# One multiplication of the score preparation on GpSimd, the state's decay behind two copies, and two buffers in place of three for a chunk's closing outputs

## The chip, the cores and the metric

The kernel runs on one core of a Trainium2 chip. The time is the device time of one execution in microseconds (us); the figure that counts is the median of several executions. Engines are called as the profile calls them: PE is the matrix engine, DVE the vector engine, ACT the scalar engine, POOL is GpSimd, SP the engine whose queue issues nearly all DMA transfers.

## The reference

Three stages follow each other: a recurrent attention with a decaying state, and two gated networks without a nonlinearity.

```python
# r, k, v: 4 x 8 x 768 x 48 (batch, head, time, dim);  w, u: 8 x 48
for t in range(S):
    cur = einsum('bhd,bhe->bhde', u[None] * kt, vt)
    y[:, :, t] = einsum('bhd,bhde->bhe', rt, state + cur)
    state = w[None, :, :, None] * state + einsum('bhd,bhe->bhde', kt, vt)
x = y as 3072 rows of 384
x = (x @ w_a * (x @ w_b)) @ w_out          # block 1: 384 -> 1536 -> 384
x = ((x @ w1 * (x @ w2)) @ w3) @ w_out2    # block 2: 384 -> 1024 -> 1024 -> 384
```

## The kernel before, in words

**Stages.** Time is cut into 6 chunks of 128 steps; a chunk of one batch row is a unit, so there are 24 units, unit u being row `u % 4` of chunk `u // 4`. A unit's attention is done in chunk form: r times powers of w (table `tr`) and k times inverse powers (`tk`) give scores by matmul; scores are masked, the diagonal gets the term with u, and the masked scores (`a_sc`) times v, plus r times the state, give y. Chunk 0 (units 0 to 3) has no state to add. For chunks 0 and 1 the preparation is `prep_0` with three multiplications of 112x512 each: part 0 is k times the table (L599), part 1 is r times the table (L602), part 2 is e = r times k (L604). They read the loaded tile `rk` and write the unit's tile `alt`. A part-1 result is wanted by the score matmuls (`scores_h`, L365 and L369), a part-2 result by the diagonal's matmuls (`scores_d`, L377, with a filler matmul L286 behind them). From chunk 2 on, L333 and L338 multiply `rk` in place on POOL.

**A unit's tail.** DVE masks the scores (L389 in chunks 0 and 1, `a_mask` later), ACT copies the part below without a mask (`h_off`, L397; from chunk 2 on `a_off`, L440, twice in a unit). Then y (L479 and L484, later `y_split`, L456), the state's sum over the chunk (L569), the state's decay by w to the 128th on ACT (`s_decay`, L576, four instructions) and the state's update on DVE (L589).

**Block 1.** A finished chunk of y (`xt`) goes through block 1 in 12 column blocks f: nine matmuls L641 for a and nine for b into PSUM banks `ab0` to `ab2`; ACT copies a into an SBUF buffer `g0`, `g1` or `g2` (L745); DVE multiplies (L746); ACT and DVE split the product in a high and a low part (L748, L751); 27 matmuls (L658 to L660) add it to the banks `m0` to `m2`. After the last f `m_close` empties the three m banks into three buffers of the same `g0` to `g2` (L720 on ACT; for chunk 0, which is done in two parts around chunk 1, L718 on DVE adds the kept part), and SP sends each to DRAM (`m_d`, L723). The weights arrive as 64-bit floats and are converted on DVE and ACT (L976, L980, L984, L989, L992, from tile `raw` to `wab`, `wo`).

**Block 2** runs after chunk 5, in another part of the program (L1202 to L1400), and the change does not touch it.

**What sets the order.** Nothing is ordered by hand: each step is a task with an engine, an assumed duration, dependences, buffers and a priority, and `plan` lays the tasks out by list scheduling on assumed times; each engine's instructions then stand in the program in that order. A DVE task marked `sbuf=True` is assumed longer while POOL is busy. A changed dependence or duration therefore also reorders work that it does not name.

```python
        if t.sbuf:
            t.dur += max(0.0, min(free.get("POOL", 0.0) - at, 2 * t.dur)) / 2
```

Of the kernel before, what the change touches and what calls it, by code (L numbers as in the profile page):

```python
# [13 lines left out]
ALU = mybir.AluOpType  # L14
# [4 lines left out]
B, H, S, D = 4, 8, 768, 48  # L19
# [149 lines left out]
def rwkv_moe_kernel(ctx, tc, rkT, nat, wu, wab, wout, w12, w3T, wo2, r_in, k_in, v_in, w_in, u_in, out):  # L169
# [10 lines left out]
    def flat(ap):  # L180
        return ap.rearrange("p a b -> p (a b)")

    with tc.manual_schedule():
# [411 lines left out]
        def prep_0(u, part):  # L595
            rk, t = rk_t[u], alt[u % B]
            rf_t[u] = t[0:112, 0].rearrange("p (n c) -> p n c", n=NP)
            if part == 0:
                nc.vector.tensor_tensor(out=t[0:112, 1].rearrange("p (n c) -> p n c", n=NP),  # L599
                                        in0=rk[:, 1, :].rearrange("p (n c) -> p n c", n=NP), in1=tk, op=ALU.mult)  # L600
            elif part == 1:
                nc.vector.tensor_tensor(out=t[0:112, 0], in0=rk[:, 0, :], in1=flat(tr), op=ALU.mult)  # L602
            elif part == 2:
                nc.gpsimd.tensor_tensor(out=t[0:112, 2], in0=rk[:, 0, :], in1=rk[:, 1, :], op=ALU.mult)  # L604
            else:
                nc.scalar.copy(out=vz_t[u % 2][:, :, :, D:],
                               in_=v_0[:, u, 6 * D:].rearrange("p (x k i) -> p k x i", x=2, k=KD))
# [64 lines left out]
        def task(*a, **k):  # L672
            t = Task(*a, **k)
            for b in t.bufs:
                b.users.append(t)
            tasks.append(t)
            return t

        def use(t, *bufs):
            for b in bufs:  # L680
                b.users.append(t)
            return t
# [172 lines left out]
        for u in range(B, NU):  # L855
            c, b = divmod(u, B)
            pu = due(28 + 8 * (u - B)) if c == 1 else due(125 + 20 * (u - 2 * B)) if c == 2 else -1000.0 + 10 * u
            rk_b[u], nat_b[u] = Buf(rk_s, none), Buf(nat_s, none)
            lr = task("SP", 0.4, lambda u=u: load_rk(u), [], pu - 100, [rk_b[u]], size=0.45)
            ln = task("SP", 0.4, lambda u=u: load_nat(u), [], pu - 100, [nat_b[u]], size=0.39 if c == 1 else 0.58)  # L860
            at_c = at_s + banks
            ba = Buf(a_s, none)
            kn = []
            if u == 2 * B:
                bt = Buf(at_c, none)
                tn = use(task("PE", 0.9, lambda bt=bt: picked([bt], tables_s), s_kn, due(82), [bt]), tmp_b)
                tn = use(task("ACT", 0.6, tables_n, [tn], due(82)), bt)
            if c < NC - 1:
                bk = Buf(kn_s, none)
                eng, d = ("DVE", 0.55) if c == 1 else ("POOL", 1.15)  # L870
                kn = s_kn = [use(task(eng, d, lambda u=u: k_nat(u), [ln, tn] + s_kn, pu, [bk]), nat_b[u])]
            if c == 1:
                bt, bd = [Buf(at_c, none) for _ in range(2)], Buf(at_c, none)
                al = alt_b[b]
                pu_ = use(task("POOL", 1.3, lambda u=u: prep_0(u, 2), [lr], pu - 9), rk_b[u], al)
                pk = use(task("DVE", 0.7, lambda u=u: prep_0(u, 0), [lr], pu - 9, sbuf=True), rk_b[u], al)
                pr = use(task("DVE", 0.7, lambda u=u: prep_0(u, 1), [lr, pk], pu - 9, sbuf=True), rk_b[u], al)
                sc = use(task("PE", 1.2, lambda u=u, bt=bt: picked(bt, lambda: scores_h(u)), [pk, pr] + after, pu, bt), al)
                sd = use(task("PE", 0.85, lambda u=u, bd=bd: picked([bd], lambda: scores_d(u)), [sc, pu_], pu, [bd]), al)
                ev = halves(u, pu - 60, sc, sd, bt, bd, ba)  # L880
                by = [Buf(at_c, none)]
                y = use(task("PE", 2.3, lambda u=u, by=by: picked(by, lambda: y_mm(u)), ev + s_up.get(u - B, []), pu + 1, by),
                        al, nat_b[u], ba)
                bs = [Buf(at_c, none)]
                sm = use(task("PE", 0.6, lambda u=u, bs=bs: picked(bs, lambda: s_mm(u)), kn + [y], pu + 2, bs), bk, nat_b[u])
                after = [y, sm]
                s_old, s_new = y, sm
            else:
                al = rk_b[u]
                t = use(task("POOL", 1.32, lambda u=u: prep_r(u, nc.gpsimd), [lr], pu - 9), rk_b[u])  # L890
                t = use(task("POOL", 1.32, lambda u=u: prep_k(u, nc.gpsimd), [t], pu - 9), rk_b[u])
                bp = Buf(pr_s, none)
                dg_b[u] = Buf(dg_s, none)
                d = use(task("POOL", 1.15, lambda u=u: prep_d(u, 0), [ln, load_u], pu - 8, [bp]), nat_b[u])
                d = use(task("POOL", 1.15, lambda u=u: prep_d(u, 1), [d], pu - 8), nat_b[u], bp)
                dg = use(task("DVE", 0.56, lambda u=u: prep_d(u, 2), [d], pu - 8, [dg_b[u]]), bp)
                by, bt = [Buf(at_s, none) for _ in range(2)], [Buf(banks, none) for _ in range(2)]
                sc = use(task("PE", 1.5, lambda u=u, bs=by + bt: picked(bs, lambda: state_scores(u)),
                              [t] + after + s_up.get(u - B, []), pu, by + bt), rk_b[u])
                of, ev = [], []  # L900
                for x in range(2):
                    ev = [use(task("DVE", 0.42, lambda u=u, x=x: a_mask(u, x), [sc] + ev, pu - 300, [] if x else [ba]), bt[x], ba)]
                    of.append(use(task("ACT", 0.28, lambda u=u, x=x: a_off(u, x), ev, pu - 300), bt[x], ba))
                ev = use(task("DVE", 0.77, lambda u=u: a_diag(u), ev + [dg], pu, sbuf=True), ba, dg_b[u])
                y = use(task("PE", 1.4 if kn else 1.1, lambda u=u: y_split(u), [ev] + of + kn, pu + 1), al, nat_b[u], ba, *by)
                if kn:
                    use(y, bk)
                after, bs = [y], by
                s_old, s_new = sc, y
            if b == 0:  # L910
                x_b[c] = Buf([x_s[X_TAG[c]]], none)
                y3_b[c] = Buf(y3_s, none)
                x_in[c] = []
            ev_y = []
            for g, d in ((None, 0.9),) if c == 1 else ((1, 0.52), (0, 0.4)):
                take = [x_b[c], y3_b[c]] if b == 0 and not ev_y else []
                yh = use(task("ACT", d, lambda u=u, g=g: y_evac_h(u, g), [y] + ev_y, pu + 2, take), by[g or 0], x_b[c], y3_b[c])
                yr = [yh]
                if c == 1:
                    yr = [use(task("PE", 0.3, lambda u=u: y_rest(u), [yh], pu + 2), by[0], x_b[c], y3_b[c])]  # L920
                yl = use(task("DVE" if c > 1 else "ACT", d, lambda u=u, g=g: y_evac_l(u, g), yr + ev_y[1:], pu + 2), by[g or 0], x_b[c], y3_b[c])
                ev_y = [yh, yl]
                x_in[c].append(yl)
            if c < NC - 1:
                sd = task("ACT", 1.56, lambda u=u: s_decay(u), [s_old], pu + 3)
                s_up[u] = [use(task("DVE", 0.85, lambda u=u: s_upd(u), [s_new, sd] + ([] if c == 1 else ev_y), pu + 3), *bs)]
            if b == B - 1:
                x_in[c].append(use(task("SP", 0.4, lambda c=c: y_shuffle(c), list(x_in[c]), pu + 3, size=0.13),
                                   x_b[c], y3_b[c]))
# [96 lines left out]
        for n, (q, fs) in enumerate([(0, range(SPLIT)), (1, range(NF1)), (0, range(SPLIT, NF1))]  # L1026
                                    + [(q, range(NF1)) for q in range(2, NB)]):
            mb = Buf(m_s, none)
            base, step = ((due(30), 80.0), (due(75), 66.0), (0.0, 10.0))[min(n, 2)]
            base += 200.0 * max(0, n - 2)  # L1030
            t_ab, t_m = block1(q, fs, base, step, x_b[q], x_in[q], mb, [m_last] if n else [])
            m_last = t_m[fs[-1]]
            if n:
                d = m_close(q, m_last, mb, base + 15 * step, g_s, g_get)
            else:
                d = [use(task("ACT", D_A, lambda k=k: m_keep(0, k), [m_last], base + 5 * step), mb) for k in range(KD)]
            if n == 2:
                mp.users = d
# [666 lines left out]
```

## Time and the profile before

| what | value |
| --- | --- |
| runs | 859.61, 860.3, 862.42 us; median 860.3 us |
| profiled execution | 860.08 us, of which the span from the first to the last instruction is 858.4 us |
| PE busy | 845.4 us of the span |
| DVE, ACT, POOL busy | 573.3, 401.2, 199.1 us |
| mean granted clock of PE | 0.998 |

The span leaves PE 13.0 us without a matmul. The 1.7 us between the span and the run's time lie outside the instructions. "Granted clock" is the share of PE's full speed that the chip granted.

### The profile page before, as it was taken

The numbers are of one execution on the slowest core, as the hardware profiler recorded it, in microseconds if no ns is written. First come the engines' busy times: TensorE is split into PE (matmuls) and PEld (weight loads), VectorE is DVE, ScalarE is ACT, GpSimd is POOL, SyncE is SP. The second block draws the span as 40 slices with busy tenths as digits, with TensorE's granted clock in tenths as the row PEclk, the third lists the DMA queues.
The fourth block names the chain that finished last, engine by engine and source line by source line (L and its number), as shares of the span: only waits on it lengthen the run. The fifth ranks groups of instructions, "written<-read, shape, count | busy, mean of one in ns | idle before, by whom it ended". The sixth has DMA issues, their size and how long they took to land.

```text
span 858.4 us, 15728 instructions
## 1 busy us (share of the span) xinstructions
PE 845.4 (98%) x5977; PEld 710.5 (83%) x5977; DVE 573.3 (67%) x1038; ACT 401.2 (47%) x961; POOL 199.1 (23%) x162
## 2 busy tenths in 40 slices
PE   9989999999999999999999999999999999999997
PEld 6778888888778888787888888888888988898887
DVE  8898976475778878654575457637658855864642
ACT  5644434465555475323367556655236222623222
POOL 4202100123544204212000202213325401511120
PEclk9999999999999999999999999999999999999999
DMA  9645732467888986722354435446445244424202
GB/s 283 191 149 158 208 116 79 150 189 207 215 226 239 269 237 195 209 77 87 86 165 134 150 123 185 139 150 239 157 132 184 87 148 134 154 71 157 92 0 78
DMA packets 71409, 134.07 MB, mean 156 GB/s; under 512 B 8032, under 2 KB 47712, under 8 KB 71328
## 3 DMA queue, kind: packets, MB, share of 16 engines
q1 hardware_dynamic: 71040, 132.61, 50.9%
q8 instruction: 49, 0.80, 0.4%
q10 hardware_dynamic: 288, 0.39, 0.1%
q14 instruction: 32, 0.26, 0.1%
HBM read 107.94 MB, written 23.07 MB: 153 GB/s over the span
## 4 chain that ended last, share of the span: by engine, by line
PE 93%; DVE 2%; DMA 1%; ACT 1%; issue 1%; SPq 0%; POOL 0%; ACTq 0%; DVEq 0%; POOLq 0%
PE ab L641 33%; PE ab L1295 14%; PE m L658 6%; PE m L659 6%; PE m L660 5%; PE at L1295 5%; PE o L1398 4%; PE at L1202 4%; PE o L1400 4%; PE o L1399 4%; PE m L286 1%; PE at L456 1%; PE at L414 1%; PE ab L423 1%; DMA wa<-w_d 1%
## 5 line engine op out<-in xcount | busy, mean ns | idle before, releaser
L746 DVE TENSOR_TENSOR ab<-g,ab 128x512 f32<-128x512 f32 x72 | 50.0, 694 | 80.4 <-PE ab L641 62.3
L1368 DVE TENSOR_TENSOR qx<-qx,ab 128x512 f32<-128x512 f32 x95 | 64.1, 685 | 36.2 <-PE ab L1295 35.7
L658 PE MATMUL m<-gh,woh 128*128 128x512 f32 x216 | 85.2, 394 | 0.0
L659 PE MATMUL m<-gl,woh 128*128 128x512 f32 x216 | 84.3, 390 | 0.0
L660 PE MATMUL m<-gh,wol 128*128 128x512 f32 x216 | 84.2, 390 | 0.0
L748 ACT CAST gh<-ab 128x512 fp32r<-128x512 f32 x72 | 42.2, 586 | 79.9 <-DVE ab L746 79.2
L745 ACT COPY g<-ab 128x512 f32<-128x512 f32 x72 | 42.0, 585 | 76.5 <-PE ab L641 72.6
L1306 POOL TENSOR_TENSOR qx<-qx,qx 128x512 f32<-128x512 f32 x29 | 39.0, 1355 | 124.9 <-DVE qx L1368 117.1
L1388 ACT CAST gh<-qx 128x512 fp32r<-128x512 f32 x48 | 29.6, 620 | 76.2 <-PE o L1399 48.7
L1362 ACT ACTIVATE qx<-ab 128x512 f32<-128x512 f32 x56 | 33.1, 598 | 56.3 <-PE ab L1295 54.8
L1390 DVE TENSOR_TENSOR gl<-qx,gh 128x512 fp32r<-128x512 f32 x48 | 37.9, 795 | 32.0 <-ACT gh L1388 30.7
L751 DVE TENSOR_TENSOR gl<-ab,gh 128x512 fp32r<-128x512 f32 x72 | 49.4, 686 | 14.1 <-ACT gh L748 13.1
L641 PE MATMUL ab<-xt,wab0h 128*128 128x512 f32 x144 | 45.9, 400 | 3.1 <-ACT g L745 1.1
L980 DVE SCALAR_TENSOR_TENSOR cvt<-raw,cvt 128x512 int32<-128x512 int32 x61 | 47.6, 781 | 1.4
L984 DVE SCALAR_TENSOR_TENSOR cvt<-raw,cvt 128x512 int32<-128x512 int32 x61 | 47.5, 779 | 1.4
L658 PEld LDWEIGHTS m<-gh,woh 128*128 128x128 f32 x216 | 40.5, 188 | 8.8
L660 PEld LDWEIGHTS m<-gh,wol 128*128 128x128 f32 x216 | 40.5, 188 | 8.5
L659 PEld LDWEIGHTS m<-gl,woh 128*128 128x128 f32 x216 | 40.5, 188 | 8.3
L641 PE MATMUL ab<-xt,wab1h 128*128 128x512 f32 x144 | 46.6, 406 | 0.0
L333 POOL TENSOR_TENSOR rk<-rk,tr 112x512 f32<-112x512 f32 x16 | 21.7, 1358 | 103.6 <-DMA rk<-in_rkT_dram 103.6
L355 POOL TENSOR_TENSOR kn<-natt,tnat 128x384 f32<-128x384 f32 x12 | 14.0, 1168 | 133.7 <-PE at L467 121.9
L641 PE MATMUL ab<-xt,wab2h 128*128 128x512 f32 x144 | 45.0, 393 | 0.0
(340 smaller groups left out, 2293.6 us busy)
## 6 DMA issues: line engine op xcount, KB each, us to landing
tg<-t_d SPq DMA_DIRECT2D x45, 640.0 KB, 3.9
raw<-in_wab_dram SPq DMA_DIRECT2D x30, 512.0 KB, 4.7
rk<-in_rkT_dram SPq DMA_DIRECT2D x24, 448.0 KB, 5.6
t_d<-part SPq DMA_DIRECT2D x75, 128.0 KB, 2.7
raw<-in_wout_dram SPq DMA_DIRECT2D x18, 512.0 KB, 4.7
natt<-in_nat_dram SPq DMA_DIRECT2D x96, 96.0 KB, 3.8
raw<-in_w3T_dram SPq DMA_DIRECT2D x16, 512.0 KB, 3.6
raw<-in_w_dram SPq DMA_DIRECT2D x12, 512.0 KB, 4.2
```

The costliest lines, as they stand in the source:

```text
L641: mm(ps, lhsT=w[i][:, k, cs], rhs=x[:, j, k, :], start=(k + i + j == 0), stop=(k == KD - 1 and i == 1))
L658: mm(m_ps[q][k], lhsT=wh[:, j, cs], rhs=gh, start=first, stop=False)
L659: mm(m_ps[q][k], lhsT=wh[:, j, cs], rhs=gl, start=False, stop=False)
L660: mm(m_ps[q][k], lhsT=wl[:, j, cs], rhs=gh, start=False, stop=last)
L745: ea = use(task("ACT", D_A, lambda x=bg, y=ba: nc.scalar.copy(out=x.ap, in_=y.ap), [a], p0 + 1, [bg]), ba)
L746: mu = use(task("DVE", D_TT, lambda x=bg, y=bb: nc.vector.tensor_tensor(out=y.ap, in0=x.ap, in1=y.ap, op=ALU.mult), [ea, b], p0 + 2), bg, bb)
L748: hi = use(task("ACT", D_A, lambda x=bh, y=bb: nc.scalar.copy(out=x.ap[0], in_=y.ap), [mu], p0 + 2, [bh]), bb)
L751: nc.vector.tensor_tensor(out=x.ap[1], in0=y.ap, in1=x.ap[0], op=ALU.subtract)
L980: nc.vector.scalar_tensor_tensor(out=t["f"], in0=t["w"][:, :, 1], scalar=-0x40000000, in1=t["f"], op0=ALU.bitwise_and, op1=ALU.bitwise_or)
L984: nc.vector.scalar_tensor_tensor(out=t["f"], in0=t["w"][:, :, 0], scalar=29, in1=t["f"], op0=ALU.logical_shift_right, op1=ALU.bitwise_or)
L1295: mm(bank, lhsT=x, rhs=y, start=(start and n == 0), stop=(stop and n == 2), skip_group_check=True)
L1368: e = use(task("DVE", D_TT, lambda bv=bv, b=bank[c], s=s: nc.vector.tensor_tensor(out=bv.ap, in0=bv.ap, in1=b.ap, op=ALU.add if s > 0 else ...
```

## The change

Three edits. (1) Part 1 of `prep_0` for units 4 to 7 (chunk 1) is issued on POOL instead of DVE, with an assumed 1.36 us, and no longer depends on part 0. (2) From chunk 2 on, `s_decay` depends on the unit's two copies `a_off`. (3) `m_close` of all but the first part of chunk 0 takes its three buffers from `g1` and `g2` alone.

```diff
@@ prep_0
             elif part == 1:
-                nc.vector.tensor_tensor(out=t[0:112, 0], in0=rk[:, 0, :], in1=flat(tr), op=ALU.mult)
+                eng = nc.vector if u < B else nc.gpsimd
+                eng.tensor_tensor(out=t[0:112, 0], in0=rk[:, 0, :], in1=flat(tr), op=ALU.mult)
@@ units of chunk 1
-                pr = use(task("DVE", 0.7, lambda u=u: prep_0(u, 1), [lr, pk], pu - 9, sbuf=True), rk_b[u], al)
+                pr = use(task("POOL", 1.36, lambda u=u: prep_0(u, 1), [lr], pu - 9), rk_b[u], al)
@@ every unit
-                sd = task("ACT", 1.56, lambda u=u: s_decay(u), [s_old], pu + 3)
+                sd = task("ACT", 1.56, lambda u=u: s_decay(u), [s_old] + (of if c > 1 else []), pu + 3)
@@ chunks of block 1
-                d = m_close(q, m_last, mb, base + 15 * step, g_s, g_get)
+                d = m_close(q, m_last, mb, base + 15 * step, g_s[1:], g_get)
```

The changed file has one line more, so that from part 1 on its line numbers are one higher (L604 becomes L605, L641 becomes L642; part 1 itself is L603).

The first place is POOL, from the first unit's e on; `alt_157` to `alt_160` are the four `alt` tiles, and `rk_196` is the load of unit 4. Before:

```order
L604 TENSOR_TENSOR alt_160<-rk_172 112x512
L604 TENSOR_TENSOR alt_157<-rk_196 112x512
L604 TENSOR_TENSOR alt_158<-rk_207 112x512
L604 TENSOR_TENSOR alt_159<-rk_476 112x512
L604 TENSOR_TENSOR alt_160<-rk_550 112x512
L333 TENSOR_TENSOR rk_628<-rk_628,tr_146 112x512
```

POOL in the changed kernel, from the same instruction to the same instruction:

```order
L605 TENSOR_TENSOR alt_160<-rk_172 112x512
L605 TENSOR_TENSOR alt_157<-rk_196 112x512
L603 TENSOR_TENSOR alt_157<-rk_196,tr_146 112x512
L605 TENSOR_TENSOR alt_158<-rk_207 112x512
L603 TENSOR_TENSOR alt_158<-rk_207,tr_146 112x512
L605 TENSOR_TENSOR alt_159<-rk_419 112x512
L603 TENSOR_TENSOR alt_159<-rk_419,tr_146 112x512
L605 TENSOR_TENSOR alt_160<-rk_517 112x512
L603 TENSOR_TENSOR alt_160<-rk_517,tr_146 112x512
L333 TENSOR_TENSOR rk_559<-rk_559,tr_146 112x512
```

Each unit of chunk 1 now has two instructions in a row on POOL, four instructions are added there, and DVE has four fewer.

The second place is PE where block 1 begins, with unit 4's diagonal (L377) ahead of it; `m_553` and `m_563` are state sums of chunk 0, `at_601` is unit 4's y. Before:

```order
L377 MATMUL ab_544<-u_x_105,alt_157 128x2 x4
L286 MATMUL ab_544<-ident_111 128x256
L569 MATMUL m_553<-v_0_99,k_0_98 48x48 x8
L569 MATMUL m_563<-v_0_99,k_0_98 48x48 x8
L641 MATMUL ab0_584<-xt_338,wab0h_383 128x512 x2
L641 MATMUL ab0_584<-xt_338,wab0l_384 128x512
L641 MATMUL ab0_584<-xt_338,wab0h_383 128x512 x2
L641 MATMUL ab0_584<-xt_338,wab0l_384 128x512
L479 MATMUL at_601<-alt_157,s0_153 112x128 x4
```

PE in the changed kernel, over the same stretch:

```order
L377 MATMUL ab_547<-u_x_105,alt_157 128x2 x4
L286 MATMUL ab_547<-ident_111 128x256
L569 MATMUL m_562<-v_0_99,k_0_98 48x48 x8
L642 MATMUL ab0_572<-xt_338,wab0h_383 128x512 x2
L642 MATMUL ab0_572<-xt_338,wab0l_384 128x512
L642 MATMUL ab0_572<-xt_338,wab0h_383 128x512 x2
L642 MATMUL ab0_572<-xt_338,wab0l_384 128x512
L569 MATMUL m_588<-v_0_99,k_0_98 48x48 x8
L479 MATMUL at_604<-alt_157,s0_153 112x128 x4
```

The second state sum moved behind the first six matmuls of block 1. On ACT beside it the two copies L397 of unit 4 stood behind the state copy L591 of unit 2 and around it; in the changed order the first L397 stands ahead of that L591. Further on, unit 5's scores move ahead of the seventh matmul L641, and unit 5's diagonal (L377, `at_695`) goes to a bank of the `at` kind in place of one of the three `ab` banks, with nine matmuls of block 1 right behind it; unit 6's diagonal follows nine matmuls of block 1 and unit 6's scores. By unit 6's L479 both orders have issued the same 48 matmuls of block 1.

The third place is ACT where chunk 1 of block 1 closes; `a_sc_1976` is a unit of chunk 2. Before:

```order
L576 ACTIVATE s1_154<-s1_154,wC_151 112x112 x4
L440 COPY a_sc_1976<-ab_1938 128x2x64
L440 COPY a_sc_1976<-ab_1939 128x2x64
L720 COPY g0_1990<-m0_1397 128x512
L720 COPY g1_2024<-m1_1398 128x512
L720 COPY g2_2027<-m2_1399 128x512
```

ACT in the changed kernel, from behind the second closing copy (`g2_2048<-m1_1396`; the first is `g1_2026<-m0_1395`) to the next unit's decay:

```order
L746 COPY g0_2065<-ab2_1979 128x512
L749 CAST gh0_2083<-ab1_2052 128x512
L746 COPY g0_2092<-ab0_2072 128x512
L956 ACTIVATE sq_2098,chk_108<-raw_1984 128x512
L959 ACTIVATE sq_2098,chk_108<-sq_2098,small_109 128x512
L721 COPY g1_2135<-m2_1397 128x512
L956 ACTIVATE sq_2139,chk_108<-raw_2024 128x512
L749 CAST gh1_2160<-ab2_2086 128x512
L440 COPY a_sc_2158<-ab_2117 128x2x64
L440 COPY a_sc_2158<-ab_2118 128x2x64
L576 ACTIVATE s2_155<-s2_155,wC_151 112x112 x4
```

The three closing copies stood together; now the third, which writes `g1` again, stands behind block 1's next two copies into `g0`. The decay L576 moved from ahead of its unit's two copies L440 to behind them. From about two thirds of the program on, PE's order is the same in both kernels.

## Rows read from the trace of the kernel before

**Rows 1.** The profile's page: busy time by engine, and the ending chain by engine.

```profile
PE 845.4 (98%) x5977; PEld 710.5 (83%) x5977; DVE 573.3 (67%) x1038; ACT 401.2 (47%) x961; POOL 199.1 (23%) x162
...
PE 93%; DVE 2%; DMA 1%; ACT 1%; issue 1%; SPq 0%; POOL 0%; ACTq 0%; DVEq 0%; POOLq 0%
```

**Rows 2.** Windows: stretch, its length, busy time of each engine, PE's clock, DMA.

```profile
60.00:240.00 180.00, 180.00 (x1559) 146.95 (x1559) 128.14 (x236) 85.72 (x212) 42.94 (x36) 1.00 0.58 163
240.00:430.00 190.00, 188.37 (x1657) 152.78 (x1656) 133.90 (x325) 88.43 (x268) 47.03 (x39) 1.00 0.62 180
430.00:585.00 155.00, 155.00 (x728) 133.71 (x727) 90.01 (x137) 96.68 (x220) 20.54 (x14) 1.00 0.44 144
```

**Rows 3.** The timeline of PE: start, duration, instruction, idle time ahead and its releaser.

```profile
34.79 0.74 PE L641 MATMUL ab<-xt,wab0h 128*128 128x512 f32 x2 [1.10 <-ACT a_sc L397]
...
47.79 0.73 PE L641 MATMUL ab<-xt,wab0h 128*128 128x512 f32 x2 [1.13 <-ACT g L745]
...
55.69 1.11 PE L377 MATMUL ab<-u_x,alt 112*128 112x2 f32 x8 [1.48 <-DVE s L589]
```

**Rows 4.** Windows behind the third gap, columns as in rows 2.

```profile
56.50:59.90 3.40, 3.40 (x10) 2.74 (x11) 2.48 (x5) 1.20 (x2) 0.00 (x0) 0.50 0.57 214
59.90:63.30 3.40, 3.40 (x42) 2.89 (x42) 3.01 (x6) 1.20 (x2) 0.00 (x0) 1.00 0.00 0
```

**Rows 5.** The timeline of DVE ahead of the three gaps.

```profile
31.34 1.55 DVE L992 TENSOR_TENSOR wab0l<-cvt,wab0h 128x512 fp32r<-128x512 f32 x1
...
43.66 1.49 DVE L976 TENSOR_SCALAR cvt<-raw 128x512 int32<-128x512 int32 x1
...
46.39 0.75 DVE L389 TENSOR_TENSOR a_sc<-at,mask_h 128x256 f32<-128x256 f32 x2
...
53.10 0.68 DVE L992 TENSOR_TENSOR wab1l<-cvt,wab1h 128x512 fp32r<-128x512 f32 x1
...
54.49 1.05 DVE L589 TENSOR_TENSOR s<-ab,s 48x96 f32<-48x96 f32 x4
```

**Rows 6.** The timeline of ACT ahead of the first gap.

```profile
33.38 0.96 ACT L591 COPY s<-m 48x96 f32<-48x96 f32 x4 [1.35 <-PE m L569]
34.37 0.63 ACT L397 COPY a_sc<-ab 64x256 f32<-64x256 f32 x2
```

**Rows 7.** By line: the three multiplications (nanoseconds min/median/max, first and last start).

```profile
L602 DVE TENSOR_TENSOR alt<-rk,tr x8: 675/681/685, 6.9 to 65.9; 112x512 f32<-112x512 f32 x8
...
L333 POOL TENSOR_TENSOR rk<-rk,tr x16: 1278/1293/1648, 41.9 to 400.4; 112x512 f32<-112x512 f32 x16
```

**Rows 8.** The timeline of POOL from 26 to 45 us.

```profile
30.64 1.70 POOL L604 TENSOR_TENSOR alt<-rk 112x512 f32<-112x512 f32 x1 [6.58 <-DMA rk<-in_rkT_dram]
...
41.89 1.30 POOL L333 TENSOR_TENSOR rk<-rk,tr 112x512 f32<-112x512 f32 x1 [3.61 <-DMA rk<-in_rkT_dram]
43.13 1.73 POOL L338 TENSOR_TENSOR rk<-rk,tr 112x512 f32<-112x512 f32 x1
```

**Rows 9.** ACT: the decay and the copies in one of the later units.

```profile
254.51 1.22 ACT L576 ACTIVATE s<-s,wC 112x112 f32<-112x112 f32 x4
255.62 0.41 ACT L440 COPY a_sc<-ab 128x128 f32<-128x128 f32 x2
```

**Rows 10.** PE's gaps at one such unit and in the last chunk.

```profile
253.56 0.45 PE L423 MATMUL ab<-rk 48*64 48x128 f32 x8 [0.49 <-ACT g L745]
...
402.93 0.73 PE L641 MATMUL ab<-xt,wab0h 128*128 128x512 f32 x2 [0.84 <-ACT a_sc L440]
```

**Rows 11.** Closes: who waits, the last sum of chunk 0, and transfer times.

```profile
179.83 0.59 ACT L745 COPY g<-ab 128x512 f32<-128x512 f32 x1 [0.85 <-DMA m_d<-g]
...
229.69 0.68 DVE L718 TENSOR_TENSOR g<-m,m_part 128x512 f32<-128x512 f32 x1
...
233.22 0.59 ACT L745 COPY g<-ab 128x512 f32<-128x512 f32 x1 [1.65 <-DMA m_d<-g]
...
DMA to landing us min/median/max: 2.0/4.8/6.8
```

## The prediction

> **What bounds the kernel now.** I read the page's busy times and its ending chain first [rows 1]: PE is busy for 845.4 of 858.4 us and carries 93% of the chain. So only three things can change the time: PE's idle 13.0 us, stretches in which PE runs at a lower clock, and new waits of PE. DVE, at 67%, has slack on the average, so taking work from it is worth something only where PE waits for it. The windows say where that is [rows 2]: from 60 to 240 us and from 430 to 585 us PE has no idle time at all, from 240 to 430 us it has 1.63 us. What is left lies before 60 us and in the tail of block 2, whose order the change leaves alone.
>
> Then the timeline of PE before 60 us. Three gaps stand there between 34 and 56 us [rows 3]: 1.10 us ahead of L641 at 34.79 (released by a copy L397), 1.13 us ahead of L641 at 47.79 (released by a copy L745), 1.48 us ahead of L377 at 55.69 (released by the state's update L589); 3.71 us together. The third is followed by something dearer than it looks: from 56.5 to 59.9 us the granted clock is 0.50, the lower of the two levels (1.2 instead of 2.4 GHz), and then 1.00 again [rows 4]. PE stood idle and then worked on the two-column matmuls L377 just before. Those 3.40 us hold the work of 1.70 us at full clock. Gaps and clock make 5.4 us to be had at the start.
>
> Last, what is behind the gaps. At the first, the ACT copy L397 that frees the bank starts at 34.37 because 0.96 us of state copies L591 stand ahead of it [rows 6]; DVE reaches the mask late as well, since L992 took 1.55 us at 31.34, while POOL's e ran from 30.64 to 32.34 [rows 5, 8]. The same L992 takes 0.68 us at 53.10, where POOL is idle [rows 5]. At the second, L976 takes 1.49 us at 43.66 beside POOL's L338 from 43.13, and the mask L389 follows only at 46.39 [rows 5, 8]. The third is DVE again: L589 runs 54.49 to 55.54 behind a conversion and a mask.
>
> **Edit 1, the multiplication.** DVE loses four instructions of 0.68 us [rows 7], 2.7 us over units 4 to 7. POOL gains four of 1.29 us, the median of the same shape in L333 [rows 7], 5.2 us in all. POOL has the room: it waited 6.58 us for unit 6's load ahead of 30.64 and 3.61 us for unit 8's ahead of 41.89 [rows 8]. The result goes to the scores, which PE reaches much later: unit 5's e lies before unit 6's at 30.64, so its r does too, while unit 5's scores stand behind block 1's first matmuls at 34.79 [rows 3, 8]. So the slower engine is not on the path.
>
> The move has a price that DVE pays: POOL beside a DVE instruction stretches it, L992 from 0.68 to 1.55, by 0.87 us [rows 5]. The new r runs right behind e, for unit 6 from about 32.3 us on. Between no stretch (2.7 us gained on DVE) and one instruction stretched by 0.87 us for each of the four (3.5 us lost against 2.7 gained: 0.8 worse) I take about even for DVE as a whole, since the row for L992 is nearer to the case than none.
>
> The Trainium skill's page "SBUF — State Buffer", section "Who interferes with whom", calls the pair of ports that DVE and GpSimd share an exclusive lock: a DVE instruction with two inputs in SBUF and a GpSimd instruction that reads SBUF wait out each other whole. By that rule the four moved multiplications block DVE for 4 x 1.29 = 5.2 us where they cost it 2.7 now, so DVE ends up to 2.5 us later. The trace agrees in kind (L992 above), and shows no stretch on the masks L389, which read PSUM.
>
> So the gain I expect comes less from DVE's load than from the order that the edit brings. In PE's order six matmuls L642 now stand between the two state sums L569, and ACT's first copy L397 stands ahead of the state copies of unit 2, not behind them. The 0.96 us of L591 [rows 6] were what made 34.37 of the copy's start, so the first gap of 1.10 us shrinks to between 0 and 0.5; I take 0.2. At the second, the bank is now asked for by nine matmuls behind unit 5's diagonal, whose scores stand earlier; what can hold them is unit 5's mask and copy behind two conversions: between 0 and twice 1.13 us, and I take 0.5. At the third, L377 no longer waits for L589 but, for unit 6, for ACT's copy of the a bank, which stands behind a weight conversion; PE has eighteen matmuls, unit 5's tail and unit 6's scores to do meanwhile, about as long, as far as rows tell, as the chain of some nine DVE instructions of up to 0.7 us and two of ACT behind the first of those matmuls. Between 0 and the 1.48 of today I take 0.3. Sum left: 1.0 us of 3.71. With 2.7 us of idle time gone and no stop of over a microsecond right at the two-column matmuls, I expect the low stretch to go too, 1.7 us. Edit 1: 2.7 + 1.7 = 4.4 us. The gain is kept, since PE from 60 to 240 us is never idle and what feeds it there hangs on PE's own progress.
>
> **Edit 2, the decay.** The four L576 take 1.22 us and stand ahead of the copies L440 [rows 9]. Letting the copies go first starts them up to 1.1 us earlier, sixteen times. But almost no wait of PE is put down to it: the gap at 402.93 released by L440 (0.84 us) is in the last chunk, where no decay exists [rows 10]. The copies are hidden by block 1's matmuls. The decayed state is wanted by the update behind the same unit's y, which itself needs the copies, so 1.2 us later costs nothing while PE is at 180.00 of 180 us [rows 2]. I take 0, with bounds of -0.5 (the gap at 253.56 [rows 10]) and +1.
>
> **Edit 3, two buffers.** A third closing copy must wait until the first copy's transfer has landed, 2.0 to 6.8 us [rows 11]. In return block 1's next copies find `g0` free: today L745 waits 0.85 and 1.65 us for a transfer at two closes [rows 11], and PE does not stop for either [rows 2]. The order puts the third copy behind two more L746, and PE has 36 matmuls of block 1 (some 7.7 us at 155 us for 728 [rows 2]) before it writes the m banks again. I take 0.
>
> **The sum.** 860.08 - 4.4 = 855.7 us in terms of the profiled execution; the median of the runs shown is 0.2 higher, so I forecast 855.8 us. With the bounds of the three waits and of the edits at nothing, its own range is 854.3 to 857.5. The runs shown differ by more than one of these terms; a difference below 0.3%, 2.6 us, could not be told from none.
>
> **The rivals.**
> *The low clock stays.* The gaps shrink, but PE still has a short stop at some diagonal and then the 3.4 us at half clock. For it: the two-column matmuls remain; against: the stop is short. 860.08 - 2.7 = 857.4 us. Chance 0.15.
> *POOL takes DVE's time.* The stretched instructions (L992 to 1.55, L976 to 1.49) come twice as often, the masks L389 stay as late as 46.39, PE loses the same 3.7 us at other places, and its clock falls as now: 859.5 to 860 us. For it: every DVE instruction beside a POOL one in rows 5 is stretched; against: the order needs the masks later. This is where the rule of the Trainium skill, taken whole, leads. Chance 0.18.
> *The third buffer is missed (slower).* At the close of chunk 0 the third sum is at 229.69, and a transfer lands only at 233.22 [rows 11]: 3.5 us, of which 1.65 is shown to be harmless. If the third copy waits so at four closes and L749 and the next banks queue behind it on ACT, 4 x 1.9 = 7.5 us are lost, 3.1 more than gained: 863.2 us. It decides once the wait of the third copy passes what PE has in banks already filled, about 1.7 us. Against: the order puts other work in between. Chance 0.10.
> *More goes than the start.* Copies ahead of the decay and a free `g0` remove 0.49, 0.84 and the like [rows 10]: 853.8 us. Chance 0.05.
>
> **How the numbers follow.** The forecast has 0.52. Faster by over 0.3% (below 857.7): the forecast, most of the low-clock rival and the last, 0.64. Same: POOL takes DVE's time, and the rest, 0.26. Slower (above 862.9): 0.10. The range leaves out the slower rival and the best: 853.3 to 860.6.
>
> **What would show it.** Right: the three gaps of rows 3 are gone or under half a microsecond, no window at clock 0.50 between 50 and 65 us, r at 1.3 to 1.7 us on POOL, and the same instruction of PE at 100 us some 4.4 us earlier. Wrong: a new wait of PE for a mask or a conversion before 60 us, with DVE instructions of over 1.4 us ahead of it; a low clock elsewhere; or L721 waiting on a transfer with PE idle behind it.

## The result and the profile after

The changed kernel takes 868.65 us (median of 5; 868.18 to 869.65), the kernel before 860.3 us. The ratio is 1.0093, with a 95% interval of 1.0077 to 1.011: slower by 0.9%, where 0.5% faster was forecast. The profiled execution took 868.65 us with a span of 866.9 us.

The page of the changed kernel, busy time by engine and the chain that ended last:

```profile
PE 848.5 (98%) x5977; PEld 712.8 (82%) x5977; DVE 569.0 (66%) x1034; ACT 400.8 (46%) x961; POOL 203.6 (23%) x166
...
PE 58%; DVE 1%; DMA 0%; ACT 0%; issue 0%; DVEq 0%
```

Against [rows 1] DVE lost its four instructions and POOL gained them. The chain's shares add to 60% only: it could be followed back to 353 us and no further, so PE's 58% is not to be set against the 93% of before. PE's own work is the same 5977 matmuls. Its busy time grew by 3.1 us, mostly at the lower clock (below); the rest of the 8.5 us of span is idle time. Windows of the changed kernel, with the stretches of [rows 2]:

```profile
60.00:240.00 180.00, 178.19 (x1509) 145.20 (x1508) 129.50 (x240) 87.04 (x216) 43.92 (x37) 1.00 0.59 168
240.00:430.00 190.00, 184.81 (x1674) 149.21 (x1673) 128.09 (x315) 86.60 (x264) 44.91 (x37) 0.99 0.61 174
430.00:585.00 155.00, 155.00 (x727) 133.74 (x727) 89.31 (x137) 91.28 (x208) 20.34 (x14) 1.00 0.46 146
```

Where PE was never idle from 60 to 240 us it now loses 1.81 us, and from 240 to 430 us 5.19 us instead of 1.63. PE's waits in the changed kernel (what was waited for: us in total, times, longest):

```profile
PE ab L642 <- ACT a_sc L440: 3.5, 2, 1.8
PE at L456 <- ACT a_sc L440: 3.2, 2, 2.1
PE at L377 <- DVE s L589: 3.1, 1, 3.1
```

Since both kernels run the same number of matmuls, the time of the n-th tells where time was lost. The 1200th stands at 135.7 us before and 136.7 after, the 1600th at 181.4 and 182.4, the 4000th at 441.2 and 449.3, the 5600th at 777.0 and 784.7. So about 1 us is lost in the first 60 us, 7.1 us between 180 and 440 us, nothing in block 2. The last matmul ends at 853.5 us before and at 860.8 after, 7.3 us later; the other 1.2 us of the span lie behind it, where the last outputs go to DRAM (6.1 us instead of 4.9 in these two executions).

**The start.** Timelines of PE, DVE and POOL, then two windows of the changed kernel:

```profile
43.33 1.84 PE L377 MATMUL at<-u_x,alt 112*128 112x2 f32 x8 [3.05 <-DVE s L589]
...
57.82 1.05 PE L377 MATMUL ab<-u_x,alt 112*128 112x2 f32 x8
...
37.96 1.76 DVE L993 TENSOR_TENSOR wab0l<-cvt,wab0h 128x512 fp32r<-128x512 f32 x1
39.65 1.76 DVE L985 SCALAR_TENSOR_TENSOR cvt<-raw,cvt 128x512 int32<-128x512 int32 x1
...
42.13 1.05 DVE L589 TENSOR_TENSOR s<-at,s 48x96 f32<-48x96 f32 x4
...
37.77 1.42 POOL L333 TENSOR_TENSOR rk<-rk,tr 112x512 f32<-112x512 f32 x1 [2.58 <-DMA rk<-in_rkT_dram]
39.14 1.72 POOL L338 TENSOR_TENSOR rk<-rk,tr 112x512 f32<-112x512 f32 x1
...
42.70:49.50 6.80, 6.17 (x19) 5.25 (x20) 3.92 (x8) 2.29 (x5) 0.00 (x0) 0.50 0.20 65
49.50:60.00 10.50, 10.50 (x124) 8.79 (x123) 8.77 (x18) 5.08 (x14) 0.00 (x0) 1.00 0.57 209
```

All three gaps of [rows 3] are gone; the third was the wait of unit 6's L377, which now starts at 57.82 without one. A new gap of 3.05 us stands in their place: unit 5's L377, which did not wait before, now takes the bank that unit 4's state update L589 empties, and L589 stands on DVE behind two conversions of 1.76 us each. Those run beside POOL's L333 and L338 of unit 8, which ran at 41.89 before [rows 8] and start at 37.77 now. From 42.7 us, still within this wait, the clock is 0.50 for 6.8 us, of which PE works for 6.2; before it was 0.50 for 3.4 us behind unit 6's L377 [rows 4].

**The later gaps.** The first of them, in the timelines of PE, ACT, DVE and POOL of the changed kernel:

```profile
228.64 0.73 PE L642 MATMUL ab<-xt,wab0h 128*128 128x512 f32 x2 [1.72 <-ACT a_sc L440]
...
228.33 0.60 ACT L440 COPY a_sc<-ab 128x128 f32<-128x128 f32 x2 [5.97 <-DVE a_sc L436]
...
227.41 0.55 DVE L348 TENSOR_REDUCE dg<-pr 128x8 f32<-128x384 f32 x1 [3.54 <-POOL pr L345]
227.88 0.75 DVE L436 TENSOR_TENSOR a_sc<-ab,mask_h 128x256 f32<-128x256 f32 x2
...
222.79 1.29 POOL L333 TENSOR_TENSOR rk<-rk,tr 112x512 f32<-112x512 f32 x1 [7.08 <-DMA rk<-in_rkT_dram]
```

Read from the bottom: the unit's load of r and k lands late, POOL starts its four instructions at 222.79, DVE's sum L348 for the diagonal waits 3.54 us for them, and the masks L436, which need nothing of it, stand behind it on DVE. So do the copies L440 on ACT, and with them the bank. The last gap, in the timelines of PE, ACT and SP, and the window behind it:

```profile
356.19 0.32 PE L456 MATMUL at<-a_sc,natt 64*48 64x128 f32 x3 [2.06 <-ACT a_sc L440]
...
355.68 0.31 ACT L1094 ACTIVATE part<-wt 128x128 fp32r<-128x128 f32 x1 [3.99 <-DMA t_d<-part]
355.89 0.25 ACT L440 COPY a_sc<-ab 128x128 f32<-128x128 f32 x1
...
349.59 3.90 SPq L557 DMA_DIRECT2D xt<-y  x6
...
356.80:360.10 3.30, 3.30 (x20) 2.58 (x14) 0.29 (x1) 0.24 (x2) 0.00 (x0) 0.50 0.68 188
```

Here the second copy L440 stands on ACT behind L1094, whose buffer is held by a transfer that SP issued only after six others, which took SP 3.90 us. Behind this wait PE ran at clock 0.50 again, for 3.3 us. At the two gaps between (1.75 us at 269.97, 1.13 at 341.87) the masks stand on DVE behind sums that are stretched beside POOL; such a pair takes 0.48 us where POOL is idle (after_tight, at 334.24 us):

```profile
265.69 2.39 DVE L1118 TENSOR_TENSOR wt<-wa 128x128 f32<-128x128 f32 x2
...
336.76 3.35 DVE L1101 SCALAR_TENSOR_TENSOR part<-wa,part 128x128 fp32r<-128x128 f32 x2
```

The four waits and the low clock make 1.72 + 1.75 + 1.13 + 2.06 + 1.65 = 8.3 us; against the 1.6 us of before that is 6.7 of the 7.1.

### The profile page after: what moved, and what is told of

Read it like the earlier page. It is cut to its first block, busy times and chain, and to the rows that moved or that the text cites. A ratio compares the mean times of both kernels' runs of the same rounds, so it can differ in the third digit from the quotient of the medians.

```text
span 866.9 us, 15714 instructions
## 1 busy us (share of the span) xinstructions
PE 848.5 (98%) x5977; PEld 712.8 (82%) x5977; DVE 569.0 (66%) x1034; ACT 400.8 (46%) x961; POOL 203.6 (23%) x166
## 4 chain that ended last, share of the span: by engine, by line
PE 58%; DVE 1%; DMA 0%; ACT 0%; issue 0%; DVEq 0%
PE ab L642 15%; PE ab L1296 14%; PE at L1296 5%; PE at L1203 4%; PE o L1399 4%; PE o L1401 4%; PE o L1400 4%; PE m L659 3%; PE m L661 3%; PE m L660 3%; DVE qx L1369 0%; PE at L456 0%; DMA t_d<-part 0%; PE at L414 0%; DVE qw5l L1289 0%; PE ab L423 0%
## 5 line engine op out<-in xcount | busy, mean ns | idle before, releaser
L642 PE MATMUL ab<-xt,wab0h 128*128 128x512 f32 x144 | 47.6, 412 | 1.8 <-ACT a_sc L440 1.7
L333 POOL TENSOR_TENSOR rk<-rk,tr 112x512 f32<-112x512 f32 x16 | 22.3, 1393 | 114.9 <-DMA rk<-in_rkT_dram 114.9
L642 PE MATMUL ab<-xt,wab3h 128*128 128x512 f32 x144 | 44.7, 391 | 1.8 <-ACT a_sc L440 1.8
L642 PE MATMUL ab<-xt,wab2h 128*128 128x512 f32 x144 | 46.0, 401 | 0.0
L642 PE MATMUL ab<-xt,wab1h 128*128 128x512 f32 x144 | 45.6, 398 | 0.0
```

The source lines that it names most:

```text
L642: mm(ps, lhsT=w[i][:, k, cs], rhs=x[:, j, k, :], start=(k + i + j == 0), stop=(k == KD - 1 and i == 1))
```

## The experiments

Each comparison is with the kernel before on the same chip; where two variants of the changed kernel are compared, their ratios to it are. "Low clock" below is the time at the lower level in an execution, worked out as 2 x (1 - mean granted clock) x span and averaged over the executions (to about 1 us, since the mean clock has three digits): 5.1 us for the kernel before, 11.1 us for the changed one. Half of it is lost where PE has work: up to 3.0 us of the difference are clock, about 5 are waits. (Some of it lies behind the last matmul and costs nothing, 1.7 us in the profiled execution of the changed kernel.)

**Each edit alone.**

```diff
# e1_only: edit 1 and nothing else
+ eng = nc.vector if u < B else nc.gpsimd
+ pr = use(task("POOL", 1.36, lambda u=u: prep_0(u, 1), [lr], pu - 9), rk_b[u], al)
# e2_only: edit 2 and nothing else
+ sd = task("ACT", 1.56, lambda u=u: s_decay(u), [s_old] + (of if c > 1 else []), pu + 3)
# e3_only: edit 3 and nothing else
+ d = m_close(q, m_last, mb, base + 15 * step, g_s[1:], g_get)
```

> Edit 1 alone (r of units 4 to 7 on GpSimd, planned there). Theory A, that each edit's loss stays where its own work lies: the first 60 us as in the changed kernel (no gap at the first block-1 matmul, one wait of about 3.0 us at unit 5's diagonal L377, then 6.8 us at clock 0.50), hence about +1.0 us at 110 us, and from there on gaps as before: 861.3 us. Rival B, that any edit makes the planner lay out a new order behind it and a new order loses several microseconds in waits by chance of where instructions come to stand: +1.0 at 110 us, and later gaps at new places, 864 to 869 us.

> Edit 2 alone (decay behind the copies of score blocks). Theory A: the first 60 us as before (three gaps, 3.4 us at clock 0.50). If the late loss of the changed kernel, some 7 us between 220 and 360 us, is the work of the decay's place, 866 to 868 us; if it is the work of edit 3, 860 us. Rival B: some other number of gaps in other places, between 858 and 868, with no decay and no copy held by another copy in them.

> Edit 3 alone (a chunk's outputs through g1 and g2). Theory A: the first 60 us as before. If the third copy's wait for the first one's transfer is what costs, PE waits behind a closing copy L720 or L718 that waits on a transfer, 3 us and more in all, 863 us or over; if it costs nothing as forecast, 860 us. Rival B: gaps at new places that name neither a closing copy nor its transfer.

Measured: edit 1 865.05 us (ratio 1.0048, 1.0028 to 1.0068; low clock 9.9 us), edit 2 863.33 us (1.0022, 1.0009 to 1.0035; 5.9 us), edit 3 861.53 us (1.001, 0.9995 to 1.0024; 5.4 us). The medians' differences add to 4.6 + 2.9 + 1.1 = 8.6 us and the ratios to 0.80% of the 0.93%, close to the whole, but not because each loses its part at its own place. PE's waits with edit 1 alone:

```profile
PE ab L642 <- ACT a_sc L440: 2.9, 3, 1.5
PE at L377 <- DVE s L589: 2.0, 1, 2.0
PE at L456 <- ACT a_sc L440: 1.6, 1, 1.6
PE ab L642 <- DVE wab0l L993: 1.1, 1, 1.1
```

Edit 1 alone, which does nothing behind 60 us, already has waits for L440 of 2.9 and 1.6 us. One of them, 0.84 us at 407, is the kernel before's own at 402.93 [rows 10]; the others, 1.48 us at 231, 1.58 at 261 and 0.57 at 358, are new and stand at other matmuls than those of the changed kernel. With edit 2 alone the largest late one is 1.61 us at 242, with edit 3 alone 1.33 us at 325. In all three no closing copy releases a wait of PE. That is rival B of the expectations, though for edits 2 and 3 its range was too wide to be much of a test: the planner lays out anew what stands behind the first place that an edit touches.

**The engine without the order.** e1_issue keeps every order of the kernel before and carries out r of units 4 to 7 on GpSimd; after_dve keeps every order of the changed kernel and carries it out on DVE.

```diff
# e1_issue, on the kernel before
-                nc.vector.tensor_tensor(out=t[0:112, 0], in0=rk[:, 0, :], in1=flat(tr), op=ALU.mult)
+                eng = nc.vector if u < B else nc.gpsimd
+                eng.tensor_tensor(out=t[0:112, 0], in0=rk[:, 0, :], in1=flat(tr), op=ALU.mult)
# after_dve, on the changed kernel
-                eng = nc.vector if u < B else nc.gpsimd
+                eng = nc.vector
```

> The planner still takes r of units 4 to 7 for a vector instruction of 0.7 us, so that every engine's order is that of the kernel before, and only the engine that carries out r is GpSimd. If the loss at the start comes from vector instructions stretched beside GpSimd, the three early gaps stay or grow and the time is 860 to 863 us. If it comes from the new order alone, taking 0.68 us off the vector engine four times shortens the gaps: 857 to 859 us. Everything behind 80 us as before in both.

> The changed kernel's plan and order, only that r of units 4 to 7 is carried out by the vector engine at the places where the plan has GpSimd do it. If the moved multiplication itself is what stretches the vector engine, its four conversions of 1.4 to 1.7 us between 28 and 34 us shrink and L377's wait falls below 1.5 us: 865 to 866.5 us. If the stretch that matters is that of unit 8's multiplications, which stay, or the order, the wait stays at 2.5 to 3.5 us: 868 to 869 us.

e1_issue: 862.0 us (1.0011, 0.9995 to 1.0027), the upper half of what the stretch theory gave, and no gain. Timelines of PE, DVE and POOL:

```profile
49.26 0.78 PE L642 MATMUL ab<-xt,wab0h 128*128 128x512 f32 x2 [2.07 <-ACT g L746]
...
43.07 1.77 DVE L993 TENSOR_TENSOR wab1l<-cvt,wab1h 128x512 fp32r<-128x512 f32 x1
44.76 1.49 DVE L977 TENSOR_SCALAR cvt<-raw 128x512 int32<-128x512 int32 x1
...
45.93 1.46 POOL L603 TENSOR_TENSOR alt<-rk,tr 112x512 f32<-112x512 f32 x1
```

Four instructions off DVE, and the second gap of [rows 3] grew from 1.13 to 2.07 us: DVE's instructions beside L333, L338 and the moved L603 are stretched. after_dve: 871.0 us (1.011, 1.0094 to 1.0126), slower than the changed kernel. Taking r back from GpSimd did not cure it: L377's wait is 1.97 us, but a wait of 1.52 us for a conversion stands two rows ahead of it, four conversions take 1.65 to 1.79 us as before, and DVE has four instructions more in front of the same deadline. 871.0 us is above both ranges that I had given, and the wait below the one that went with the slower of them. So taking r off GpSimd alone is no remedy; it does not show that the moved multiplication is harmless, since DVE has to do it instead. The place of unit 8's is tested next.

**Unit 8's multiplications held back.** L333 and L338 of unit 8 are issued behind a copy of one element that reads unit 4's updated state; nothing else moves.

```diff
# after_pool_late (a new tile tok) and after_pool (the old tile warm), on the changed kernel
+        def late_8(u, f):
+            if u == 2 * B and held != [None]:
+                held.append(f)
+            else:
+                f()
...
+            if u == B:     # in s_upd, behind the update of unit 4's state
+                nc.gpsimd.tensor_copy(out=warm, in_=s_t[0][0:1, 0, 0:1])
+                for f in held: f()
```

> The changed kernel with every engine's order kept; only GpSimd's two multiplications of unit 8 (L333, L338) are made to wait for unit 4's state update, so that they no longer run beside the vector instructions ahead of it. If stretched vector instructions are what delays unit 5's diagonal, the conversions at 38 to 41 us fall from 1.76 to 0.69 us each, the wait of L377 from 3.05 to about 0.9 us, the low clock behind it from 6.8 to 3.4 us or less: 864 to 866.5 us. If the new bank of L377 and the order are at fault, the wait stays near 3 us and the time near 868.6 us.

> The edit of after_pool_late once more, without the new 4-byte tile that the first version put ahead of all others on chip (its one-element copy now goes into a tile that was there). In the first version the wait of L377 was 1.3 us in place of 3.05 and PE stood 1.8 us earlier at the 800th matmul, but the matmuls of block 2 ran slower throughout. If the tile's 4 bytes made that slowness, block 2 runs as in the changed kernel and the early gain stays: 865 to 867 us. If the wait itself or GpSimd's copy made it, 873 to 875 us again.

after_pool_late: 874.9 us (1.0165, 1.0152 to 1.0179), outside both expectations. The wait of L377 fell to 1.3 us and PE stood 1.8 us earlier at the 800th matmul, but later it lost time steadily in stretches without a wait, 4.5 us between the 4000th and the 5600th matmul. That pointed at the new tile. after_pool, without it: 866.18 us (1.0072, 1.0051 to 1.0093), as the stretch theory said. That interval still overlaps the changed kernel's; the trace is clearer: PE stands 3.7 us earlier at the 1200th matmul. Timelines of DVE, POOL and PE of after_pool (line numbers are 17 higher there):

```profile
38.62 0.68 DVE L1010 TENSOR_TENSOR wab0l<-cvt,wab0h 128x512 fp32r<-128x512 f32 x1
39.21 0.69 DVE L1002 SCALAR_TENSOR_TENSOR cvt<-raw,cvt 128x512 int32<-128x512 int32 x1
...
41.06 1.26 POOL L333 TENSOR_TENSOR rk<-rk,tr 112x512 f32<-112x512 f32 x1
...
41.83 1.02 PE L377 MATMUL at<-u_x,alt 112*128 112x2 f32 x8 [0.81 <-DVE s L606]
```

The two conversions are back at 0.68 and 0.69 us, and L377's wait falls from 3.05 to 0.81 us. The low clock falls from 11.1 to 7.5 us. The later waits stay (4.3 and 1.7 us for L440), and two new ones for L769 (0.83 us at 89, 1.07 at 197) take some of the gain back.

**The tile alone.**

```diff
# before_shift, on the kernel before
+        tok = const.tile([1, 1], F32, name="tok")
+        nc.gpsimd.memset(tok, 0.0)
```

> The kernel before with one more 4-byte tile, set once and never read, ahead of all later tiles on chip. If the place of the tiles alone slows PE, block 2 is longer by some 4 us and the time is 864 to 868 us; if not, 860.4 us.

The tile comes with one instruction that sets it. 870.5 us (1.0131, 1.0109 to 1.0153): four bytes that nobody reads cost 10 us, more than the upper end of what I gave. It settles after_pool_late; more below.

**Copies right at their masks.** Every engine's plan is kept; the copy is issued in the mask's place, and the sum L348 right ahead of the step that reads it or of the next unit's products on POOL, whichever comes first.

```diff
# after_tight on the changed kernel, before_tight on the kernel before
-  ev = [use(task("DVE", 0.42, lambda u=u, x=x: a_mask(u, x), ...
-  of.append(use(task("ACT", 0.28, lambda u=u, x=x: a_off(u, x), ev, ...
+  ev = [use(task("DVE", 0.42, lambda u=u, x=x: (a_mask(u, x), a_off(u, x)), ...
+  of.append(use(task("ACT", 0.28, lambda: None, ev, ...
-  dg = use(task("DVE", 0.56, lambda u=u: prep_d(u, 2), [d], ...
+  dg = use(task("DVE", 0.56, lambda u=u: red.append(u), [d], ...
-  lambda u=u: a_diag(u), ev + [dg], ...
+  lambda u=u: (reduce_now(), a_diag(u)), ev + [dg], ...
```

> The changed kernel with the matmuls' order kept; from chunk 2 on each copy of score blocks is issued right behind its mask, and the sum for the diagonal right ahead of the step that reads it, so that neither stands behind another unit's instruction that waits for a transfer. If the late loss is made by instructions that stand in order behind such a waiting one, the waits at 228.6 us (1.7) and 356.2 us (2.1, and 3.4 us at clock 0.50 behind it) go, those at 270 and 342 us, where the mask itself stands behind sums on the vector engine, stay: 863 to 865.5 us. If the loss hangs on the decay's place or the closing buffers, which are as in the changed kernel, it stays near 868.6 us.

> The same edit on the kernel before. It has one wait released by such a copy (0.84 us at 402.9) and 0.49 us at 253.6: 859 to 860.4 us, if nothing new stands in the way.

after_tight: 862.41 us (1.0024, 1.001 to 1.0038), 6.2 us better than the changed kernel and a little under the range: the two gaps that I expected to stay went too. Why those two went is not shown: sums stretched beside POOL are still there (one takes 2.62 us at 255), but ahead of no wait. Nor did I separate the copies from the sums. PE's waits in after_tight (L385 is L377, L405 is L397, L451 the diagonal's step):

```profile
PE at L385 <- DVE s L597: 2.0, 1, 2.0
PE at L464 <- DVE a_sc L451: 1.1, 1, 1.1
PE ab L650 <- ACT a_sc L405: 0.5, 1, 0.5
```

The waits for L440 are gone. The decay still has its place behind the copies in the plan and the closing copies still use two buffers, so neither was the cause by itself. The start is about as bad as in the changed kernel (1.96 us at L377 and 0.93 for a conversion, 9.8 us at low clock). before_tight: 860.21 us (1.0003, 0.9992 to 1.0014): there the order already had hardly such waits, and the remedy is worth nothing.

**Both remedies, on four kernels.** after_tight_pool has all three edits, before_tight_pool none, e1_tight_pool edit 1, e23_tight_pool edits 2 and 3; each has both changes shown above.

> Both edits on the changed kernel: copies and diagonal sums right at their masks, unit 8's GpSimd work behind unit 4's state update. If stretched vector instructions at the start and copies behind waiting instructions later are the two causes of the loss, what is left is the changed kernel without its loss: 858.5 to 861 us. If the low clock at the start (about 10 us of the span at 0.50 on the average) stays, 861 to 862.5 us.

> The same two edits on the kernel before. Its second early gap (1.1 us) stands behind a conversion stretched to 1.49 us by unit 8's GpSimd work; freed of it the gap falls to about 0.2 us, the rest as in before_tight: 858 to 859.8 us. If what GpSimd leaves undone at 42 us is late for unit 8, 860 to 862 us.

> Edit 1 with both remedies (copies and diagonal sums at their masks, unit 8's GpSimd work behind unit 4's state update). If the gain of 2.2 us in after_tight_pool is edit 1's order at the start, 857.5 to 859 us; if edits 2 and 3 are part of it, 859.5 us and over.

> Edits 2 and 3 with both remedies. If edit 1 carries the gain, the start is that of the kernel before and the time 859.5 to 861 us; if edits 2 and 3 carry it, 858 to 859 us; if their new order still costs, 861.5 us and over.

Measured: after_tight_pool 858.23 us, a little under its range (0.9978, 0.9965 to 0.9992; low clock 5.7 us); before_tight_pool 860.39 us (1.0, 0.9988 to 1.0012); e1_tight_pool 858.98 us against 861.13 us of the kernel before in that series (0.9968, 0.9952 to 0.9984; low clock 4.0 us); e23_tight_pool 859.13 us (0.9985, 0.9971 to 0.9999), between its ranges. Holding back unit 8's multiplications is worth more here than in after_pool: after_tight_pool and after_tight differ by that edit alone, and their intervals lie apart. For before_tight_pool I missed: the second gap, at 48 us, grew from 1.13 to 1.68 us, since there L333 stood just behind that update anyway: held back it starts at 42.27 us instead of 41.89 and meets the same two DVE instructions, stretched to 1.73 and 1.48 us. PE's waits and the windows of after_tight_pool:

```profile
PE at L464 <- DVE a_sc L451: 2.0, 1, 2.0
PE m L286 <- POOL ident L272: 1.5, 1, 1.5
PE at L385 <- DVE s L614: 0.8, 1, 0.8
PE ab L667 <- DVE gl L777: 0.6, 1, 0.6
...
42.00:50.00 8.00, 8.00 (x84) 6.90 (x84) 7.87 (x14) 4.33 (x11) 1.61 (x1) 1.00 0.40 108
...
240.00:430.00 190.00, 190.00 (x1667) 154.27 (x1666) 131.41 (x324) 89.40 (x266) 44.41 (x37) 1.00 0.63 181
```

With the stretch and the queueing gone, PE is never idle from 240 to 430 us in this execution and its clock is full where it was 0.50. That execution ran at a mean clock of 0.999; over all executions the low clock is 5.7 us, no less than that of the kernel before. The three edits then make the kernel 0.2% faster, which is below what I set as the least to tell from no change, though its interval excludes 1. In the traces the gain stands at the start and comes with edit 1: the 1600th matmul is at 178 us in after_tight_pool and e1_tight_pool, at 181 us in e23_tight_pool and the kernel before. That edits 2 and 3 add or take anything is not shown: the interval of e23_tight_pool lies just below 1 as well, and the three overlap. These versions are the fastest here; the later wait of 2.0 us, for the diagonal sum behind a late load, is what they have left.

## Why the prediction was wrong

**What bounds the kernel** was read rightly: what is gained or lost in these runs is PE's idle time or PE's clock, save for 1.2 us behind the last matmul of the changed kernel and for the two runs with one more tile, whose matmuls are slower themselves.

**Edit 1, the three gaps** were expected to leave 0.2, 0.5 and 0.3 us; all three are gone, the first by the order named.

**Edit 1, the wait of unit 5's diagonal** is the first failed step: it has no term in the sum. I priced L377's wait at 0.3 us, "between 0 and the 1.48 of today", for the diagonal of unit 6. Unit 5's diagonal, which the order had moved to another bank, was the one to follow: it waits 3.05 us for the reader of that bank. Today's waits bounded the old places only; none of them is a bound for an instruction that is given another thing to wait for.

**The price of the move on DVE** is the step beneath it. I looked for the stretch beside the four moved multiplications and called it even. The two traces show what I passed over: unit 8's two multiplications come 4.1 us earlier (41.89 to 37.77), since its load goes out earlier, and fall on the conversions ahead of L589. Held back in after_pool, they give 2.2 us of the wait back. The rule of the Trainium skill, page "SBUF — State Buffer", section "Who interferes with whom", that DVE with two SBUF inputs and GpSimd wait each other out whole, would put a GpSimd instruction's 1.29 us where I took 0.87. The trace agrees in kind: the conversions lost 1.76 - 0.69 = 1.07 us each, between the two, and with edit 2 alone a conversion that began beside one GpSimd instruction was held through the next one too, which my price of one stretch did not allow for (timelines of DVE and POOL):

```profile
237.28 2.80 DVE L980 SCALAR_TENSOR_TENSOR cvt<-raw,cvt 128x512 int32<-128x512 int32 x1
...
237.00 1.28 POOL L333 TENSOR_TENSOR rk<-rk,tr 112x512 f32<-112x512 f32 x1 [3.91 <-DMA rk<-in_rkT_dram]
238.25 1.28 POOL L338 TENSOR_TENSOR rk<-rk,tr 112x512 f32<-112x512 f32 x1
```

The rival that the Trainium skill's rule led to ("POOL takes DVE's time") was right in kind and wrong in place and size.

**The clock**: the 1.7 us I booked as gain became a loss of 1.4 us, since PE works for 6.2 us at 0.50 instead of 3.4. In the profiled executions the low stretch behind L377's wait lasted 6.8 us after waits of 1.96, 1.97 and 3.05 us; 3.4 us, 6.8 us or nothing after waits of 1.5 us; 3.4 us after one of 1.3 us; and there was none after waits of 0.8 and 0.9 us. It also varies between executions of one kernel (from none to 10.3 us in all for the kernel before), and the kernel before took 858.54 to 864.45 us in one series.

**The order behind the start, taken as unchanged** (edits 2 and 3 at nothing, and edit 1's gain kept to the end) is the second failed step, and the larger: 7.1 us lie behind 180 us, where I had written that "the gain is kept, since PE from 60 to 240 us is never idle". That idle-free stretch belonged to the order of before. I had read how the planner moved instructions at the places that the edits name and taken the rest as unchanged. The runs with one edit each, edit 1 too, show new gaps at matmuls of their own, and after_tight shows what made most of them in the changed kernel: the copy or the mask that frees a bank stands, on an engine that takes its instructions in the order of the program, behind one that waits for a transfer. For the two gaps behind stretched sums this is read from the timelines and not tested by itself. The plan's assumed times know neither the 3.35 us of two stretched sums nor the 3.90 us that SP spends on the six transfers, for which it has 0.4.

**The slower rival** had the right sign and the wrong mechanism: no closing copy releases a wait of PE in any run. The third buffer cost 1.1 us in e3_only, within what that interval calls no change.

**The sum.** The three upper bounds (0.5, 2.26 and 1.48 us) and edit 2's +1 stand 4.2 us above the values taken, so that "its own range" ended at 860.0 us and not at 857.5. And the 0.64 for faster counts only 0.07 of the low-clock rival's 0.15, not most of it. Neither reaches the measured time.

**The gain that was argued for exists**: at the 1600th matmul after_tight_pool stands at 178.1 us, 3.3 us ahead of the kernel before. It needs both remedies to reach the end.

## What to carry to other kernels

Where a planner sets the order, an edit's price is not at the edit: compare the whole order, and ask of each instruction that frees a bank what it stands behind and whether that can wait for a transfer. A stretch without idle time in the old profile is no cover for a new order. Work moved to GpSimd is to be judged by when all of GpSimd's work then runs, the next unit's too, since what it meets on DVE pays for it; and an issue in another place with the plan kept (as in after_pool and after_tight) tests such a wait without a new order.

## What the runs showed of the hardware

Four bytes more on chip, ahead of the tiles that are allocated later, slow the kernel by 1.3%. The same three matmuls of block 1, in the timelines of PE of before_shift and then of the kernel before:

```profile
480.68 0.62 PE L643 MATMUL ab<-xt,wab0h 128*128 128x512 f32 x2
481.14 0.40 PE L643 MATMUL ab<-xt,wab0l 128*128 128x512 f32 x1
481.38 0.63 PE L643 MATMUL ab<-xt,wab0h 128*128 128x512 f32 x2
```

```profile
476.12 0.62 PE L641 MATMUL ab<-xt,wab0h 128*128 128x512 f32 x2
476.57 0.39 PE L641 MATMUL ab<-xt,wab0l 128*128 128x512 f32 x1
476.80 0.62 PE L641 MATMUL ab<-xt,wab0h 128*128 128x512 f32 x2
```

Three take 0.70 us instead of 0.68 without a wait, and between 430 and 585 us PE gets through 718 matmuls instead of 728 while busy all the time at full clock. The kernel begins with a tile of padding, which this fits. Which operand's address counts, and at what step, was not tried.
